# Experts two to four of a dense mixture on six tiles of 384 tokens in place of eight of 288

## The chip, the cores and the metric

One core of one Trainium2 chip runs the whole program. The metric is the device time of one execution in microseconds; lower is better. Several executions are timed and their median is given; one further execution was recorded by the hardware profiler, and every row below is from that one.

## The reference, cut to what matters

Three parts follow each other. B is 4 batches, S 576 tokens, 8 heads of 64; there are 2304 tokens of 512 features, E is 4 experts of width 1024, and the last layer has width 2048.

```
p_packed = attention(p, k, v)                # 32 packed queries a head
x = attention(q, p_packed, p_packed)         # 2304 x 512
p = domain_probs / (domain_probs.sum(-1) + 1e-9)
for e in range(4):                           # every token goes through every expert
    h = max(x @ w1[e], 0)
    out += p[:, e] * (h @ w2[e])
h = out @ w_in
g = P(h) / (Q(h) + 1e-6)                     # a cubic over a quadratic in |h|
y = g @ w_out
```

## The kernel before, in words

**Precision.** Each float32 operand of a large product is split into a rounded high part and a low part (both of the type fp32r), and a product is three matmuls: high by high, low weight by high, high by low.

**Folded weights.** The second attention's output is not formed. Its probabilities, 32 a head, are kept for all tokens in `aH` and `aL` (two groups of 128 rows, 2304 columns), and the packed values of a batch are multiplied into an expert's first weights. So the first product of expert e works with a weight `wb[e, bb]` that is different for each batch `bb`, and has two groups of 128 rows to sum over. `st_wb` (line 138) builds one half of such a weight (16 matmuls at line 147, a rounding copy by ScalarE at line 149) and `st_wbl` (line 134) its low part (VectorE, line 136). Two `wb` buffers exist; one accumulator area of two banks serves the builds (line 473).

**Units.** The expert stage is a list of 256 units (line 475): expert, batch, half of a batch (288 tokens), and one of eight chunks of 128 of the expert's width. For each unit `emit_h` (line 526) issues 6 matmuls of 288 columns into one of two banks (line 471): two groups by three. VectorE then applies the maximum with zero and the token's weight (line 558), ScalarE rounds (line 559), GpSimd forms the low part (line 560). Three units later `emit_out` (line 641) issues the second product of that unit, 12 matmuls of 288 columns (line 639): four accumulator banks, one for each 128 output features, by three. After eight chunks `emit_acc` (line 685) moves the four banks into the accumulator `acc` in SBUF: a copy by ScalarE for expert one, a sum by VectorE (line 695) for the others.

```
units = [("m", e, bb, a_, c) for e in range(E) for bb in range(B) for a_ in range(2) for c in range(NCH1)]
for i, (w, x) in enumerate(ops):
    nc.tensor.matmul(ps[:, :n], w, x, start=(i == 0), stop=(i == len(ops) - 1))
```

**Order.** All is written out by hand, one step a unit. A step's order on TensorE is: the first product of unit kk, then the second product of unit kk - 3, then whatever `at_step` (lines 512 to 517) put after it: the attention of the following batches and the builds of folded weights in expert one, then one build of two halves per batch, at the steps 4 and 10 of the 16 steps of a batch (line 516), each followed one step later by its low part. Beside this run the loading and splitting of the second weights (`put_w2`, line 119), of the token weights (`load_pw`, line 219, one row of 288 broadcast to all partitions, one tile ahead), and of the next expert's raw first weights.

**Conversion.** `w_in` and `w_out` come as 64-bit floats. `narrowing` (line 161) converts them in 32 tasks to two fp32r parts in DRAM; a task is cut in seven pieces: a load on SP's queue, four pieces with two VectorE instructions each (lines 193 to 205), one with a rounding by ScalarE and a subtraction by GpSimd, one with two stores. From step 41 on, two pieces are taken in each step (line 775), none in the steps where an accumulator is emptied or near a change of expert.

**Last stage.** 96 units of 384 tokens by 128 of the width of 2048: 12 matmuls of 384 columns (line 548), a chain over VectorE (lines 578, 579 and 592), ScalarE and GpSimd for the rational function, and four units later 9 matmuls of 512 columns (line 639). Its inputs are split from `acc` (`emit_x2`, line 701), its weights read back by `put_final` (line 128).

Of the kernel before, what the change touches and what calls it, by code (L numbers as in the profile page):

```python
# [8 lines left out]
F32 = mybir.dt.float32  # L9
F32R = mybir.dt.float32r  # L10
# [3 lines left out]
ALU = mybir.AluOpType  # L14
# [5 lines left out]
def kernel(ctx, tc, q, k, v, p, probs, w1, w2, w_in, a, b, w_out, out):  # L20
    nc = tc.nc
    B, H, S, D = q.shape
    NT, E = probs.shape
# [3 lines left out]
    P = 128  # L27
    KC = DM // P
# [3 lines left out]
    HALF = S // 2  # L32
    KP = 96
    NKC = S // KP
    NJ = NKC // 2
    TOK = 384
# [3 lines left out]
    NCH1 = F1 // P  # L40
    NCH2 = F2 // P
    FH = 512
    LAGF = 4

    const = ctx.enter_context(tc.tile_pool(name="const", bufs=1))
    wp = ctx.enter_context(tc.tile_pool(name="wp", bufs=NCH1))
    hp = ctx.enter_context(tc.tile_pool(name="hp", bufs=4))
# [5 lines left out]
    pwp = moe.enter_context(tc.tile_pool(name="pwp", bufs=2, side="right"))  # L53
# [4 lines left out]
    with tc.manual_schedule():  # L58
# [49 lines left out]
        wb = {}  # L108
# [108 lines left out]
        pw = {}  # L217

        def load_pw(n):

            if n < E * B * 2:
                w = pw[n] = pwp.tile([P, HALF], F32, tag="pw", name="pw")
                nc.sync.dma_start(out=w, in_=prow[n * NJ:(n + 1) * NJ, :].rearrange("(o s) n -> o (s n)", o=1).to_broadcast([P, HALF]))

# [245 lines left out]
        ps_acc = ctx.enter_context(tc.tile_pool(name="ps_acc", bufs=KC, space=PSUM, reuse_waits="tile"))  # L472
        apt = tc.tile_pool(name="apt", bufs=1, space=PSUM, side="right", reuse_waits="tile")
        banks[0] = apt.__enter__()
        units = [("m", e, bb, a_, c) for e in range(E) for bb in range(B) for a_ in range(2) for c in range(NCH1)]
        NUM = len(units)
        units += [("f", pr, c, tt) for pr in range(NPAIR) for c in range(NCH2) for tt in range(2)]
        NU = len(units)
        PH = 2 * NCH1


        side = {}

        def at_step(kk, w, f, *args):
            side.setdefault((kk, w), []).append((f, args))
# [25 lines left out]
        ATT = (B - 2) * PACE + 15  # L511
        for c in range(2, NCH1):
            at_step(c - 1, 1, put_w2, 0, c)
        for ph in range(B - 1, E * B - 1):
            for fh in range(2):
                at_step(ph * PH + 4 + 6 * fh, 1, st_wb, (ph + 1) // B, (ph + 1) % B, fh)
                at_step(ph * PH + 5 + 6 * fh, 0, st_wbl)
        tail = ExitStack()
        cvt = iter(())
        tp = None  # L520
# [5 lines left out]
        def emit_h(u):  # L526
            ps = ps_h.tile([P, 512], F32, tag="h", name="h")
            ops = []
            if u[0] == "m":
                _, e, bb, a_, c = u  # L530
                n = HALF
                w = wb[e, bb]
                cols = slice(bb * S + a_ * HALF, bb * S + (a_ + 1) * HALF)
                for g in range(2):
                    wh, wl = (w[:, x, g, c * P:c * P + P] for x in range(2))
                    ops += [(wh, aH[:, g, cols]), (wl, aH[:, g, cols]), (wh, aL[:, g, cols])]
            else:
                _, pr, c, tt = u
                n = TOK
                w = wts["f", pr * NCH2 + c, 0]  # L540
                xh, xl = xs[2 * pr + tt]
                for kc in range(KC):
                    wh, wl = (w[:, x, kc * P:kc * P + P] for x in range(2))
                    ops += [(wh, xh[:, kc, :]), (wl, xh[:, kc, :]), (wh, xl[:, kc, :])]
            if u == units[0]:
                keep(ps[:, :P], 44)
            for i, (w, x) in enumerate(ops):
                nc.tensor.matmul(ps[:, :n], w, x, start=(i == 0), stop=(i == len(ops) - 1))  # L548
            ph = ps[:, :n]
            if u[0] == "m":  # L550
                t = (e * B + bb) * 2 + a_
                if c == 0:
                    load_pw(t + 1)
                hw = hp.tile([P, HALF], F32, tag="hw", name="hw", bufs=2)
                hh = hp.tile([P, HALF], F32R, tag="hh", name="hh")
                hl = hp.tile([P, HALF], F32R, tag="hl", name="hl")
                hs[u] = (hh, hl)
                nc.vector.scalar_tensor_tensor(out=hw, in0=ph, scalar=0.0, in1=pw[t], op0=ALU.max, op1=ALU.mult)  # L558
                nc.scalar.copy(out=hh, in_=hw)  # L559
                nc.gpsimd.tensor_tensor(out=hl, in0=hw, in1=f32(hh), op=ALU.subtract)  # L560
                return
            m = tp.tile([P, TOK], F32, tag="m", name="m")
            c1 = tp.tile([P, TOK], F32, tag="c1", name="c1")
            c0 = tp.tile([P, TOK], F32, tag="c0", name="c0")
            nc.scalar.activation(out=c1, in_=ph, func=AF.Identity, scale=a_sb[:, 3:4], bias=a_sb[:, 2:3])
            nc.scalar.activation(out=m, in_=ph, func=AF.Abs, scale=b_abs[:, 0:1])
            nc.scalar.activation(out=c0, in_=ph, func=AF.Identity, scale=a_sb[:, 1:2], bias=a_sb[:, 0:1])

            nc.scalar.activation(out=ph, in_=ph, func=AF.Square)  # L569
            nc.scalar.activation(out=m, in_=m, func=AF.Identity, bias=one)  # L570
            mid[u] = (m, ph, c1, c0)
# [65 lines left out]
        def products(ps, n, ops, first, last):  # L637
            for i, (w, x) in enumerate(ops):
                nc.tensor.matmul(ps[:, :n], w, x, start=(first and i == 0), stop=(last and i == 2))  # L639

        def emit_out(u):
            hh, hl = hs.pop(u)
            if u[0] == "m":
                _, e, bb, a_, c = u
                wh, wl = (wts[e, c][:, x, :] for x in range(2))
                if c == 0:
                    accs["m"] = [ps_acc.tile([P, 512], F32, tag="acc", name="acc") for _ in range(KC)]
                for s, ps in enumerate(accs["m"]):
                    o = slice(s * P, s * P + P)

                    products(ps, HALF, ((wh[:, o], hh), (wh[:, o], hl), (wl[:, o], hh)), c == 0, c == NCH1 - 1)
                if c == NCH1 - 1:
                    late.append((u, accs["m"]))
            else:
                _, pr, c, tt = u
                wh, wl = (wts["f", pr * NCH2 + c, 1][:, x, :] for x in range(2))
                if c == 0:
                    accs[tt] = [(ps_y if tt and s else ps_acc).tile([P, 512], F32, tag="acc", name="acc") for s in range(SUB)]
                for s, ps in enumerate(accs[tt]):
                    o = slice(s * P, s * P + P)  # L660

                    products(ps, DM, ((hh[:, o], wh), (hl[:, o], wh), (hh[:, o], wl)), c == 0, c == NCH2 - 1)
                if c == NCH2 - 1:
                    late.append((u, accs[tt]))
# [20 lines left out]
        def emit_acc():  # L685
            while late:
                u, bks = late.pop(0)
                for s, ps in enumerate(bks):
                    if u[0] == "m":
                        _, e, bb, a_, c = u  # L690
                        dst = acc[bb][:, s, a_ * HALF:(a_ + 1) * HALF]
                        if e == 0:
                            nc.scalar.copy(out=dst, in_=ps[:, :HALF])
                        else:
                            nc.vector.tensor_tensor(out=dst, in0=ps[:, :HALF], in1=dst, op=ALU.add)
                        continue
                    store(u, s, ps)
                if u[0] == "m" and u[1] == E - 1:
                    done_cols[0] += HALF

        def emit_x2(t, bb, c0, n, o, kc):
            hi, lo = (x[:, kc:kc + 2, o:o + n] for x in xs[t])
# [21 lines left out]
        def refill(u, j):  # L724

            if u[0] == "m":
                _, e, bb, a_, c = u
                if j == 1 and bb == B - 1 and a_ == 1:
                    if e + 1 < E:
                        put_w2(e + 1, c)  # L730
                    else:
                        put_final(c // 2, c % 2)
            else:
                _, pr, c, tt = u
                n = pr * NCH2 + c + NCH1 // 2
                if tt == 1 and n < NPAIR * NCH2:
                    put_final(n, j)

        for kk in range(NU):
            if kk == ATT:  # L740
# [1 line left out]
                accp2 = ctx.enter_context(tc.tile_pool(name="accp2", bufs=1, reuse_waits="tile"))  # L742
                acc += [accp2.tile([P, KC, S], F32, name=f"acc{i}") for i in range(2, B)]
                cvt = narrowing(tail.enter_context(tc.tile_pool(name="cv", bufs=2, reuse_waits="tile")))
            if kk == NUM - 3 * PH:
                for _ in cvt:
                    pass
                tail.close()
                xp0 = ctx.enter_context(tc.tile_pool(name="xp0", bufs=1, reuse_waits="tile"))
                for t in range(2):  # L750
                    xs[t] = [xp0.tile([P, KC, TOK], F32R, name=f"x{nm}{t}") for nm in "HL"]
# [20 lines left out]
            emit_acc()  # L772


            for _ in range(0 if kk % NCH1 == 2 or (B * PH - 5 <= kk % (B * PH) or kk % (B * PH) < 5) else 2):
                next(cvt, None)
            if todo and todo[0][0] <= done_cols[0] and (kk < NUM or kk % 2 == 0) and todo[0][1][0] in xs:
                emit_x2(*todo.pop(0)[1])
# [43 lines left out]
```

## Time and profile before

| what | us |
|---|---|
| median of three executions | 1145.38 |
| lowest and highest of them | 1144.23, 1145.69 |
| the profiled execution, its own time | 1144.21 |
| its span, first to last instruction of the program | 1142.4 |
| TensorE's matmuls busy in the span | 1119.4 |
| VectorE, ScalarE, GpSimd busy | 756.6, 542.3, 628.5 |

In a row of the timeline the first number is the start in us from the span's start and the second the time from the first start to the last end of what was merged in that row; two starts are apart by that time less the duration of the last one. Matmuls overlap: one of 288 columns is shown with about 295 ns from its start to its modelled end, while its successor starts earlier. PE is the matmuls and PEld the weight loads, both on TensorE. "h" is the result of a first product, "acc" of a second, "wb" of a build of folded weights. Arrows in brackets name what ended the idle time before an instruction.

### The profile page before, as it was taken

How to read it: one execution, taken by the hardware profiler on the slowest of the kernel's cores; microseconds unless marked ns; L12 is line 12 of the kernel's file. 1: busy time of each engine (PE TensorE's matmuls, PEld its weight loads, DVE VectorE, ACT ScalarE, POOL GpSimd, SP SyncE). 2: the span in 40 equal slices, each digit the busy share in tenths (PEclk: the TensorE clock that was granted, in tenths of full speed). 3: DMA queues.
4: the chain of work that ended last, by engine and by line, in shares of the span. 5: the costliest groups of instructions: out<-in, count | busy, mean ns of one | idle time of the engine just before them, and what ended most of it. 6: DMA issues, size and time to landing. Idle time of an engine off the chain costs nothing.

```text
span 1142.4 us, 20688 instructions
## 1 busy us (share of the span) xinstructions
PE 1119.4 (98%) x8163; PEld 1025.5 (90%) x8163; DVE 756.6 (66%) x1061; ACT 542.3 (47%) x1085; POOL 628.5 (55%) x664
## 2 busy tenths in 40 slices
PE   8899999999999999999999999999999999999997
PEld 6678889999999999999999999988998999999996
DVE  3443436728888657878452332578888988888886
ACT  4443443342222332222322221577778777787774
POOL 0543434464445564444645333487877777777774
PEclk9899999999999999999999999999999999999999
DMA  9543214332344333344300000533333534354321
GB/s 259 132 125 88 69 48 127 129 98 89 113 153 145 103 113 116 106 153 133 112 25 11 6 7 6 186 111 120 137 113 122 191 119 138 113 169 144 125 98 55
DMA packets 61920, 125.93 MB, mean 110 GB/s; under 512 B 6960, under 2 KB 29488, under 8 KB 61824
## 3 DMA queue, kind: packets, MB, share of 16 engines
q1 hardware_dynamic: 61504, 123.79, 34.7%
q8 instruction: 64, 1.05, 0.4%
q0 software_dynamic: 320, 0.82, 0.2%
q14 instruction: 32, 0.26, 0.1%
HBM read 103.06 MB, written 21.53 MB: 109 GB/s over the span
## 4 chain that ended last, share of the span: by engine, by line
PE 91%; DVE 3%; ACT 2%; issue 2%; POOL 2%; POOLq 0%; ACTq 0%; DVEq 0%
PE acc L639 50%; PE h L548 34%; PE wb L147 3%; PE tr L293 1%; PE s L302 1%; DVE m L579 1%; PE e1t L327 1%; PE h L251 0%; PE pp L339 0%; POOL m L586 0%; POOL hl L601 0%; ACT e L315 0%; POOL c L593 0%; DVE mx L310 0%; PE pT L251 0%
## 5 line engine op out<-in xcount | busy, mean ns | idle before, releaser
L639 PE MATMUL acc<-hh,w 128*128 128x288 f32 x2048 | 449.6, 296 | 0.0
L560 POOL TENSOR_TENSOR hl<-hw,hh 128x288 fp32r<-128x288 f32 x256 | 211.7, 829 | 331.9 <-ACT hh L559 331.7
L639 PEld LDWEIGHTS acc<-hh,w 128*128 128x128 f32 x2048 | 341.5, 188 | 9.3 <-issue 9.3
L639 PE MATMUL acc<-hl,w 128*128 128x288 f32 x1024 | 301.1, 294 | 0.0
L559 ACT CAST hh<-hw 128x288 fp32r<-128x288 f32 x256 | 110.4, 431 | 381.3 <-DVE hw L558 379.4
L558 DVE SCALAR_TENSOR_TENSOR hw<-h,pw 128x288 f32<-128x288 f32 x256 | 116.1, 454 | 263.7 <-PE h L548 255.7
L579 DVE RECIPROCAL m<-m 128x384 f32<-128x384 f32 x95 | 242.5, 2553 | 3.2
L548 PE MATMUL h<-aH,wb 128*128 128x288 f32 x1024 | 216.9, 300 | 0.0
L548 PE MATMUL h<-xH,w 128*128 128x384 f32 x768 | 197.0, 337 | 3.0 <-DVE m L578 3.0
L639 PE MATMUL acc<-w,hh 128*128 128x512 f32 x576 | 194.8, 393 | 0.2 <-ACT hh L630 0.2
L639 PEld LDWEIGHTS acc<-hl,w 128*128 128x128 f32 x1024 | 192.4, 188 | 0.0
L548 PEld LDWEIGHTS h<-aH,wb 128*128 128x128 f32 x1024 | 163.1, 188 | 24.7 <-issue 10.7
L548 PEld LDWEIGHTS h<-xH,w 128*128 128x128 f32 x768 | 140.5, 188 | 13.0 <-DVE m L578 5.4
L548 PE MATMUL h<-aL,wb 128*128 128x288 f32 x512 | 151.4, 296 | 0.0
L586 POOL TENSOR_TENSOR m<-m,c 128x384 f32<-128x384 f32 x94 | 95.8, 1019 | 72.4 <-DVE m L579 72.4
L548 PE MATMUL h<-xL,w 128*128 128x384 f32 x384 | 129.5, 337 | 0.0
L639 PEld LDWEIGHTS acc<-w,hh 128*128 128x128 f32 x576 | 108.2, 188 | 21.2 <-ACT hh L630 0.7
L639 PE MATMUL acc<-w,hl 128*128 128x512 f32 x288 | 113.9, 396 | 0.0
L593 POOL TENSOR_TENSOR c<-c,c 128x384 f32<-128x384 f32 x96 | 97.9, 1020 | 5.2 <-DVE c L592 3.8
L601 POOL TENSOR_TENSOR hl<-m,hh 128x384 fp32r<-128x384 f32 x94 | 95.6, 1017 | 7.2 <-ACT hh L587 7.2
L548 PEld LDWEIGHTS h<-aL,wb 128*128 128x128 f32 x512 | 96.5, 188 | 0.1
L592 DVE TENSOR_TENSOR c<-h,c 128x384 f32<-128x384 f32 x96 | 52.5, 547 | 51.5 <-ACT h L569 51.4
(110 smaller groups left out, 1290.6 us busy)
## 6 DMA issues: line engine op xcount, KB each, us to landing
w<-nw SPq DMA_DIRECT2D x96, 512.0 KB, 4.2
r<-in_moe_w_dram SPq DMA_DIRECT2D x32, 256.0 KB, 2.7
raw<-in_moe_w_in_dram SPq DMA_DIRECT2D x16, 512.0 KB, 4.6
raw<-in_moe_w_out_dram SPq DMA_DIRECT2D x16, 512.0 KB, 3.8
nw<-raw SPq DMA_DIRECT2D x32, 256.0 KB, 2.3
nw<-t SPq DMA_DIRECT2D x32, 256.0 KB, 2.6
r<-in_moe_w_dram SPq DMA_DIRECT2D x7, 1024.0 KB, 5.6
pw<-prow SPq DMA_DIRECT2D x32, 144.0 KB, 3.7
```

What stands on the lines that cost most here:

```text
L147: nc.tensor.matmul(ps[32 * c:32 * c + 32, g, :], bd[r, 2 * bb + g, 32 * c:32 * c + 32], raw1[fh][r, c, f], start=True, stop=True, tile_pos ...
L293: nc.tensor.transpose(ps[:, hh, c * KP:c * KP + KP], src[2 * j + hh][:, c * 2 * D:(c + 1) * 2 * D], ident[:KP, :KP])
L548: nc.tensor.matmul(ps[:, :n], w, x, start=(i == 0), stop=(i == len(ops) - 1))
L558: nc.vector.scalar_tensor_tensor(out=hw, in0=ph, scalar=0.0, in1=pw[t], op0=ALU.max, op1=ALU.mult)
L559: nc.scalar.copy(out=hh, in_=hw)
L560: nc.gpsimd.tensor_tensor(out=hl, in0=hw, in1=f32(hh), op=ALU.subtract)
L579: nc.vector.reciprocal(out=m, in_=m)
L586: nc.gpsimd.tensor_tensor(out=m, in0=m, in1=c1, op=ALU.mult)
L592: nc.vector.tensor_tensor(out=c1, in0=s, in1=c1, op=ALU.mult)
L593: nc.gpsimd.tensor_tensor(out=c1, in0=c1, in1=c0, op=ALU.add)
L601: nc.gpsimd.tensor_tensor(out=hl, in0=m, in1=f32(hh), op=ALU.subtract)
L639: nc.tensor.matmul(ps[:, :n], w, x, start=(first and i == 0), stop=(last and i == 2))
```

## The change

The list of units is made from tiles of tokens: for expert one eight tiles of 288 as before, for each of the other three six tiles of 384 that don't keep to batches (`TOK` is 384, `HALF` 288, `S` 576, `NT` 2304). Tiles 1 and 4 of the six lie in two batches, 192 tokens in each; there the first product is two series of 6 matmuls with 192 columns, one with each batch's folded weight, into the two parts of one bank. Everything after that works on all 384 columns at once, but for the sum into `acc`, which is kept by batch. The builds of folded weights move to steps 3 and 5 of tiles 0, 2, 3 and 5. The conversion takes three pieces a step from expert two on.

```
+    tiles = [(0, c0, HALF) for c0 in range(0, NT, HALF)] + [(e, c0, TOK) for e in range(1, E) for c0 in range(0, NT, TOK)]
...
-            if n < E * B * 2:
-                w = pw[n] = pwp.tile([P, HALF], F32, tag="pw", name="pw")
-                nc.sync.dma_start(out=w, in_=prow[n * NJ:(n + 1) * NJ, :].rearrange("(o s) n -> o (s n)", o=1).to_broadcast([P, HALF]))
+            e, c0, m = tiles[n]
+            r0 = (e * NT + c0) // KP
+            w = pw[n] = pwp.tile([P, m], F32, tag="pw", name="pw")
+            nc.sync.dma_start(out=w, in_=prow[r0:r0 + m // KP, :].rearrange("(o s) n -> o (s n)", o=1).to_broadcast([P, m]))
...
-        units = [("m", e, bb, a_, c) for e in range(E) for bb in range(B) for a_ in range(2) for c in range(NCH1)]
+        units = [("m", n, c) for n in range(len(tiles)) for c in range(NCH1)]
         NUM = len(units)
+        begin = [NCH1 * [t[0] for t in tiles].index(e) for e in range(E)] + [NUM]
+
+        def pieces(n):
+
+            _, c0, w = tiles[n]
+            at, got = c0, []
+            while at < c0 + w:
+                k_ = min(c0 + w - at, S - at % S)
+                got.append((at // S, at % S, at - c0, k_))
+                at += k_
+            return got
...
-        for ph in range(B - 1, E * B - 1):
-            for fh in range(2):
-                at_step(ph * PH + 4 + 6 * fh, 1, st_wb, (ph + 1) // B, (ph + 1) % B, fh)
-                at_step(ph * PH + 5 + 6 * fh, 0, st_wbl)
+
+        for fh in range(2):
+            at_step((2 * B - 2) * NCH1 + 4 + 6 * fh, 1, st_wb, 1, 0, fh)
+            at_step((2 * B - 2) * NCH1 + 5 + 6 * fh, 0, st_wbl)
+        for e in range(1, E):
+            for n, e2, bb in ((0, e, 1), (2, e, 2), (3, e, 3), (5, e + 1, 0)):
+                for fh in range(2 if e2 < E else 0):
+                    at_step(begin[e] + n * NCH1 + 3 + 2 * fh, 1, st_wb, e2, bb, fh)
+                    at_step(begin[e] + n * NCH1 + 4 + 2 * fh, 0, st_wbl)
...
-                _, e, bb, a_, c = u
-                n = HALF
-                w = wb[e, bb]
-                cols = slice(bb * S + a_ * HALF, bb * S + (a_ + 1) * HALF)
-                for g in range(2):
-                    wh, wl = (w[:, x, g, c * P:c * P + P] for x in range(2))
-                    ops += [(wh, aH[:, g, cols]), (wl, aH[:, g, cols]), (wh, aL[:, g, cols])]
+                _, t, c = u
+                e, c0, n = tiles[t]
+                for bb, _, o, m in pieces(t):
+                    w = wb[e, bb]
+                    cols = slice(c0 + o, c0 + o + m)
+                    for g in range(2):
+                        wh, wl = (w[:, x, g, c * P:c * P + P] for x in range(2))
+                        ops += [(slice(o, o + m), g == 0 and i == 0, g == 1 and i == 2, wx, x)
+                                for i, (wx, x) in enumerate(((wh, aH[:, g, cols]), (wl, aH[:, g, cols]), (wh, aL[:, g, cols])))]
...
-            for i, (w, x) in enumerate(ops):
-                nc.tensor.matmul(ps[:, :n], w, x, start=(i == 0), stop=(i == len(ops) - 1))
+            for o, first, last, w_, x in ops:
+                nc.tensor.matmul(ps[:, o], w_, x, start=first, stop=last)
...
-                    products(ps, HALF, ((wh[:, o], hh), (wh[:, o], hl), (wl[:, o], hh)), c == 0, c == NCH1 - 1)
+                    products(ps, n, ((wh[:, o], hh), (wh[:, o], hl), (wl[:, o], hh)), c == 0, c == NCH1 - 1)
...
-                        dst = acc[bb][:, s, a_ * HALF:(a_ + 1) * HALF]
-                        if e == 0:
-                            nc.scalar.copy(out=dst, in_=ps[:, :HALF])
-                        else:
-                            nc.vector.tensor_tensor(out=dst, in0=ps[:, :HALF], in1=dst, op=ALU.add)
+                        for bb, at, o, n in pieces(u[1]):
+                            dst = acc[bb][:, s, at:at + n]
+                            if tiles[u[1]][0] == 0:
+                                nc.scalar.copy(out=dst, in_=ps[:, o:o + n])
+                            else:
+                                nc.vector.tensor_tensor(out=dst, in0=ps[:, o:o + n], in1=dst, op=ALU.add)
...
-            for _ in range(0 if kk % NCH1 == 2 or (B * PH - 5 <= kk % (B * PH) or kk % (B * PH) < 5) else 2):
+            for _ in range(0 if kk % NCH1 == 2 or any(-5 <= kk - x < 5 for x in begin[1:]) else 2 if kk < begin[1] else 3):
                 next(cvt, None)
```

The other lines of the diff rename what a unit is made of. The list has 208 units of the experts after the change, 64 of expert one and 48 of each other.

## Rows read from the trace of the kernel before

**Rows 1.** The page: busy time of TensorE, and the chain by engine.

```profile
PE 1119.4 (98%) x8163; PEld 1025.5 (90%) x8163; DVE 756.6 (66%) x1061; ACT 542.3 (47%) x1085; POOL 628.5 (55%) x664
...
PE 91%; DVE 3%; ACT 2%; issue 2%; POOL 2%; POOLq 0%; ACTq 0%; DVEq 0%
```

**Rows 2.** Busy time by stretch: expert two (instructions; PEclk, DMA share, GB/s last).

```profile
241.00:402.70 161.70, 161.70 (x1282) 153.70 (x1281) 120.10 (x210) 47.40 (x98) 82.48 (x86) 1.00 0.38 119
```

**Rows 3.** Waits of the weight loads, 241.06 to 723.7: total, times, longest.

```profile
PEld h L548 <- DVE acc L695: 9.2, 11, 0.8
PEld h L548 <- issue: 6.7, 8, 0.8
```

**Rows 4.** Timeline of TensorE's matmuls: experts two to four, and four units within.

```profile
241.06 0.43 PE L548 MATMUL h<-aH,wb 128*128 128x288 f32 x2
...
400.38 0.30 PE L548 MATMUL h<-aH,wb 128*128 128x288 f32 x1
...
409.88 0.29 PE L548 MATMUL h<-aH,wb 128*128 128x288 f32 x1
...
723.75 0.52 PE L548 MATMUL h<-xH,w 128*128 128x384 f32 x2
```

**Rows 5.** Groups by form, 241.06 to 723.7: busy, mean ns, idle before.

```profile
L147 PE MATMUL wb<-r,bd 64*32 64x512 f32 x352 | 24.0, 601 | 0.0
```

**Rows 6.** The chain in order of time, last stage: start, us.

```profile
787.35 2.10 PE h L548 x12
789.46 2.08 PE acc L639 x9
...
858.52 2.10 PE h L548 x12
```

**Rows 7.** Timeline of the weight loads: with nothing streaming, and in the stream.

```profile
26.96 0.20 PEld L251 LDWEIGHTS h<-ident 128*128 128x128 f32 x2 [0.51 <-PE s L302]
...
31.72 0.30 PEld L548 LDWEIGHTS h<-aH,wb 128*128 128x128 f32 x2
...
402.64 0.32 PEld L548 LDWEIGHTS h<-aH,wb 128*128 128x128 f32 x2
...
1135.12 0.19 PEld L639 LDWEIGHTS acc<-w,hl 128*128 128x128 f32 x1
1135.22 0.19 PEld L639 LDWEIGHTS acc<-w,hh 128*128 128x128 f32 x1
```

**Rows 8.** Groups by form, whole span: work beside TensorE.

```profile
L558 DVE SCALAR_TENSOR_TENSOR hw<-h,pw 128x288 f32<-128x288 f32 x256 | 116.1, 454 | 263.7 <-PE h L548 255.7 <-POOL t L378 2.6 <-POOL xL L705 1.9
...
L592 DVE TENSOR_TENSOR c<-h,c 128x384 f32<-128x384 f32 x96 | 52.5, 547 | 51.5 <-ACT h L569 51.4
...
L695 DVE TENSOR_TENSOR acc<-acc,acc 128x288 f32<-128x288 f32 x96 | 37.7, 450 | 0.0
L136 DVE TENSOR_TENSOR wb<-wb 128x1024 fp32r<-128x1024 f32 x31 | 37.5, 1211 | 3.4 <-ACT wb L149 3.4
...
L149 ACT CAST wb<-wb 128x1024 fp32r<-128x1024 f32 x31 | 31.5, 1016 | 33.3 <-PE wb L147 33.2
```

**Rows 9.** Timeline at the last stage's start: VectorE, then TensorE.

```profile
732.99 2.55 DVE L579 RECIPROCAL m<-m 128x384 f32<-128x384 f32 x1
735.46 1.49 DVE L695 TENSOR_TENSOR acc<-acc,acc 128x288 f32<-128x288 f32 x4
736.87 0.55 DVE L592 TENSOR_TENSOR c<-h,c 128x384 f32<-128x384 f32 x1
...
737.99 0.44 PE L548 MATMUL h<-xH,w 128*128 128x384 f32 x1 [1.01 <-DVE m L578]
```

**Rows 10.** Groups by form, whole span: VectorE's heavier pieces of the conversion.

```profile
L200 DVE SCALAR_TENSOR_TENSOR u<-u,t 128x512 int32<-128x512 int32 x32 | 29.9, 933 | 0.6
L205 DVE TENSOR_TENSOR u<-u,t 128x512 f32<-128x512 f32 x32 | 27.3, 852 | 1.1
...
L204 DVE SCALAR_TENSOR_TENSOR t<-raw,t 128x512 f32<-128x512 uint32 x32 | 23.2, 724 | 0.6
L202 DVE TENSOR_SCALAR t<-u 128x512 int32<-128x512 int32 x32 | 22.9, 714 | 1.1
```

More of the change, by code (lines that the diff above doesn't have):

```diff
@@ L474 @@
         banks[0] = apt.__enter__()
-        units = [("m", e, bb, a_, c) for e in range(E) for bb in range(B) for a_ in range(2) for c in range(NCH1)]
+        units = [("m", n, c) for n in range(len(tiles)) for c in range(NCH1)]
         NUM = len(units)
+        begin = [NCH1 * [t[0] for t in tiles].index(e) for e in range(E)] + [NUM]
[7 more added lines that the diff above has]
+            return got
         units += [("f", pr, c, tt) for pr in range(NPAIR) for c in range(NCH2) for tt in range(2)]
         NU = len(units)
-        PH = 2 * NCH1
         side = {}
@@ L543, in emit_h @@
                     wh, wl = (w[:, x, kc * P:kc * P + P] for x in range(2))
-                    ops += [(wh, xh[:, kc, :]), (wl, xh[:, kc, :]), (wh, xl[:, kc, :])]
+                    ops += [(slice(0, n), kc == 0 and i == 0, kc == KC - 1 and i == 2, w_, x)
+                            for i, (w_, x) in enumerate(((wh, xh[:, kc, :]), (wl, xh[:, kc, :]), (wh, xl[:, kc, :])))]
             if u == units[0]:
                 keep(ps[:, :P], 44)
-            for i, (w, x) in enumerate(ops):
-                nc.tensor.matmul(ps[:, :n], w, x, start=(i == 0), stop=(i == len(ops) - 1))
+            for o, first, last, w_, x in ops:
+                nc.tensor.matmul(ps[:, o], w_, x, start=first, stop=last)
             ph = ps[:, :n]
             if u[0] == "m":
-                t = (e * B + bb) * 2 + a_
-                if c == 0:
+                if c == 0 and t + 1 < len(tiles):
                     load_pw(t + 1)
-                hw = hp.tile([P, HALF], F32, tag="hw", name="hw", bufs=2)
-                hh = hp.tile([P, HALF], F32R, tag="hh", name="hh")
-                hl = hp.tile([P, HALF], F32R, tag="hl", name="hl")
+                hw = hp.tile([P, n], F32, tag="hw", name="hw", bufs=2)
+                hh = hp.tile([P, n], F32R, tag="hh", name="hh")
+                hl = hp.tile([P, n], F32R, tag="hl", name="hl")
                 hs[u] = (hh, hl)
@@ L643, in emit_out @@
             if u[0] == "m":
-                _, e, bb, a_, c = u
+                _, t, c = u
+                e, _, n = tiles[t]
                 wh, wl = (wts[e, c][:, x, :] for x in range(2))
@@ L689, in emit_acc @@
                     if u[0] == "m":
-                        _, e, bb, a_, c = u
-                        dst = acc[bb][:, s, a_ * HALF:(a_ + 1) * HALF]
-                        if e == 0:
-                            nc.scalar.copy(out=dst, in_=ps[:, :HALF])
-                        else:
-                            nc.vector.tensor_tensor(out=dst, in0=ps[:, :HALF], in1=dst, op=ALU.add)
+                        for bb, at, o, n in pieces(u[1]):
[4 more added lines that the diff above has]
+                                nc.vector.tensor_tensor(out=dst, in0=ps[:, o:o + n], in1=dst, op=ALU.add)
                         continue
                     store(u, s, ps)
-                if u[0] == "m" and u[1] == E - 1:
-                    done_cols[0] += HALF
+                if u[0] == "m" and tiles[u[1]][0] == E - 1:
+                    done_cols[0] += tiles[u[1]][2]
         def emit_x2(t, bb, c0, n, o, kc):
@@ L726, in refill @@
             if u[0] == "m":
-                _, e, bb, a_, c = u
-                if j == 1 and bb == B - 1 and a_ == 1:
+                _, t, c = u
+                e, c0, n = tiles[t]
+                if j == 1 and c0 + n == NT:
                     if e + 1 < E:
@@ L744 @@
                 cvt = narrowing(tail.enter_context(tc.tile_pool(name="cv", bufs=2, reuse_waits="tile")))
-            if kk == NUM - 3 * PH:
+            if kk == begin[E - 1] + 2 * NCH1:
                 for _ in cvt:
```

## The prediction

> **What bounds the kernel now.** I read the page first, for the engine that is never idle. TensorE is busy for 98% of the span and carries 91% of the chain that ended last [rows 1], so what its stream of products takes is what the program takes, as long as nobody keeps it waiting. Second I read the three experts that the change touches, as stretches: in the first of them TensorE is busy for all of its 161.70 us at a granted clock of 1.00, which is the 2.4 GHz level, while VectorE has 120.10 us of work, three quarters [rows 2]. Third the waits: TensorE's matmuls wait for nobody in the three experts, and the weight loader's longest pauses, 0.8 us [rows 3], stand where the eight-part products of the folded weights stream and no load is due. So this stage is a pure stream, and the question is what one product in it costs.
>
> That is read from the timeline. Experts two to four run from the first product of expert two at 241.06 to the first of the last stage at 723.75, 482.69 us [rows 4]. Four units of 18 products with 288 columns go from 400.38 to 409.88 [rows 4], 2.375 us a unit, 131.9 ns a product; 192 units make 456.0 us. The other 26.7 us are the 22 builds of folded weights (352 products, 16 each [rows 5]), 1.21 us each.
>
> The last stage gives a second point. A unit there is 12 products of 384 columns and 9 of 512, and 17 such units go from 787.35 to 858.52 in the chain [rows 6], 4.1865 us each. With a product's time as a + b times its columns, 18a + 5184b = 2.375 and 21a + 9216b = 4.1865 give b = 0.447 ns and a = 3.2 ns. So a product of 384 columns takes 174.8 ns (the 2.10 us shown for twelve of them [rows 6] agree), and one of 192 would take 89.0 ns if only its columns counted. A product's fixed share is tiny, 3 ns: fewer, wider products have little to win.
>
> **What the row of the weight loads adds.** Each product has its own load of 128 columns ahead of it. In the stream the loads start 0.13 us apart (two in 0.32 us, one lasting 0.19 [rows 7]), at the pace of the products, so this doesn't show what a load needs. It shows where nothing streamed: at 31.72 two loads start 0.11 us apart (two in 0.30 us, one lasting 0.19 [rows 7]), though only the first product was to start in between. From there to the pair at 1135.12 [rows 7] 94 pairs are so, at 107 to 111 ns to the nanosecond, 109 in the mean. The second load can't start until the first product has taken over the first weights, and that product is waiting for them: about 109 ns is what one load occupies. For 288 columns (132 ns) and more it is hidden behind the product before it. For 192 (89 ns) it isn't. The nearest row for a cheaper load is that of the plain transposes at 26.96, where the second starts 0.06 us after the first [rows 7]; those load the identity unrounded, in the transposing mode, and the products of the experts don't.
>
> **The change part by part.**
>
> *Products.* Before: 192 units of 18, 3456 products of 288, 456.0 us. After: each of three experts has six tiles of eight units. Four tiles lie in one batch: 18 products of 384. Two lie across a boundary: 12 of 192 in the first product, 12 of 384 in the second. That makes 2304 of 384, 2304 x 174.8 ns = 402.8 us, and 576 of 192. Bounds of a halved product: 89 ns by columns, 111 ns by the slowest pair of loads; I take 109 ns, since the rows of the same kind of load all say so, and 107 to 111 for the range. 576 x 109 ns = 62.8 us. Sum 465.6 us, **+9.6 us** (+8.4 to +10.7). Counting columns alone it would be 454.1 us, -1.9 us.
>
> By the Trainium skill ("TensorE: Matmul & The Clock Gate", Back-to-back issue gap) the spacing of warm matmuls is the columns over 2.4 GHz plus 2.5 ns, and a sustained stream of load and matmul pairs still makes 81 ns at 128 columns; both would put 192 columns well below 109 ns. Its formula gives 122.5 ns for 288 columns where the trace has 131.9, and by it the products would take 421.9 us in place of 423.4, a gain of 1.5 us. No run here shows its case of 128 columns with a load ahead of each.
>
> *Builds of folded weights.* 22 before and after (eight for expert two, eight for three, six for four), at other steps: no change. The two halves come two units apart where they were six, and share one bank: the second must wait until ScalarE and VectorE have read the first, 1.02 and 1.21 us [rows 8], with two units of over 3.1 us to do it in. If the cover went, each of 11 second halves would pay up to that, 2.2 us.
>
> *Vector work per unit.* The weighting goes from 64 instructions of 454 ns an expert to 48 at about 0.55 us (547 ns for another one of 384 columns [rows 8]), the cast and the subtraction likewise. The sum into the accumulator is four of 0.55 us in a plain tile, eight of about 0.35 us (from 450 ns at 288 columns and 547 at 384 [rows 8], 1 ns a column) in a split one, 2.8 us where 1.8 stood. It starts bank by bank while the last second product still runs (2.1 us) and the next tile's first second product comes after a first product of 1.05 us or more, so each bank is free 1 us ahead: hidden. If not, 6 tiles x 0.5 us = 3 us.
>
> *Conversion of the last stage's weights.* Three pieces a step in place of two from expert two on, in steps of 3.1 us in place of 2.4: the same load, to within a tenth, on an engine with a quarter free [rows 2]. It ends earlier, by the end of expert three. A raw tile is loaded again only after its predecessor was stored, and three steps, 9.4 us, lie between; on SP's queue the rows of token weights (one load a tile, of 384 now and then, ahead by one tile of 25 us) stand behind no more than before, and nothing else there is moved but the raw first weights, which have two tiles. Cost 0, up to +3.
>
> *Entry of the last stage.* The last three second products of expert four run between the first units of that stage: 3 x 12 x 43 ns = +1.5 us, already in the sum. VectorE is busy there: a reciprocal from 732.99 to 735.5, then the four sums into the accumulator from 735.46, then the next unit's work at 736.87, and TensorE's next product at 737.99 after 1.01 us idle [rows 9]. After the change the second products end at 12.6 us from the stage's start where they ended at 11.0, and the reciprocal at 12.3 in place of 11.8, since its unit's first product comes 0.5 later; the four sums (2.2 us, bank by bank) end at 14.5, and with 1.05 us for the next two vector instructions the product starts at 15.5 where it started at 14.24: +1.3 for +1.5. So -0.25 us, from -1.5 (all swallowed) to +1.
>
> Sum: **+9.3 us**. The profiled execution took 1144.21 us, 1.2 under the median of the three runs, 1145.38; that makes 1153.5 for it and **1154.7 us** for the median, 0.8% slower. What counts as a difference at all is 0.2%, 2.3 us.
>
> **Rivals.**
> - *The load stays hidden, not slower (0.10).* If a load can begin while the one before it is still waiting to be used, halves cost 89 ns: -1.9 - 0.25, 1143.2 us, on the edge between no change and faster. It decides at the 576 halves, and at 109 ns against 89. For it: the straight line through 288, 384 and 512 columns. Against it: 94 pairs that never start closer than 107 ns with an empty array. The Trainium skill's sustained 81 ns at 128 columns (same page and section) is this rival.
> - *VectorE's queue takes over (0.05).* The first product of a unit needs the bank that was read by the weighting two units back; from the end of one first product there are 2.10 + 1.05 + 2.10 = 5.25 us. Three pieces of conversion, two of them 0.93 + 0.71 and 0.72 + 0.85 us [rows 10] and a third at most like the lighter of these, make 4.8 us, with the weighting 5.35, and 1.2 us of folded weights on top in 16 steps of experts two and three. If each of those kept TensorE waiting for 0.8 us, 13 us more: 1167.5 us. Against it: three quarters of load, and after a heavy bunch come pieces with no vector work.
> - That the halves be merged again can't be: they have different weights.
>
> **How the numbers follow.** Forecast 0.85, first rival 0.10 (of which 0.07 within 0.2% and 0.03 faster by more), second 0.05. Slower by over 0.2%: 0.85 + 0.05 = 0.90. The range holds the forecast's case alone: low end +8.4 - 1.3 at the entry, 1152.5; high end +10.7 + 1 at the entry and some 1.4 of queueing, 1158.5. The first rival's time lies outside, with 0.10, and the second's with 0.05.
>
> **What would show it.** Halved products 107 to 111 ns apart, a split unit at 3.40 us and a plain one at 3.15 us; experts two to four at 492 us in place of 482.7; TensorE still without a wait there; and the stretch from the last stage's start to its fifth unit longer by 1.3 us. Halves 89 ns apart would make the forecast wrong, as would pauses of TensorE ahead of a first product that VectorE ends.

## The result, and the profile after

The change takes 1155.11 us in the median of five runs (1153.81 to 1156.35) where the kernel before takes 1145.69 us in five runs beside it: a ratio of 1.0082 (95% interval 1.0071 to 1.0093), slower. The forecast was 1154.7 us, between 1152.5 and 1158.5. In a later set the two stood at 1153.95 and 1145.47 us, 1.0071 (1.0059 to 1.0084).

The profiled execution took 1156.35 us with a span of 1154.5, 12.1 more than before. Of these 2.7 lie ahead of everything that was changed: the first product of expert one started at 34.5 us where it had started at 31.7, and in the eleven profiles of this study it lies anywhere from 31.7 to 34.8, with nothing altered ahead of it but sizes of buffers and, in three of the runs, one load of raw weights. In this execution 1.9 of the 2.7 are 44 transposes just ahead of that product: they start 0.11 us apart before, and here for a good part 0.21, in a stretch where the granted clock is 0.50 (27.75 to 31.70), which is the level of 1.2 GHz. So I compare stretches, not spans. These are the ends of the stretch that was changed (timeline of TensorE's matmuls of the changed kernel; they answer to [rows 4] and [rows 9]):

```profile
243.22 0.51 PE L570 MATMUL h<-aH,wb 128*128 128x384 f32 x2
...
734.00 0.51 PE L570 MATMUL h<-xH,w 128*128 128x384 f32 x2
...
749.14 0.45 PE L570 MATMUL h<-xH,w 128*128 128x384 f32 x1 [0.41 <-DVE m L599]
```

Experts two to four take 490.78 us in place of 482.69, +8.1. From their start to the fifth unit of the last stage, where the last three second products are done as well, it is 505.92 us in place of 496.93 (241.06 to 737.99): **+9.0 us**. The rest, +3.1 in this execution, is the start and half a microsecond either way elsewhere.

Where the 9 us are is seen in the chain in order of time, at the step from a plain tile to a split one (start, us, instructions):

```profile
266.22 1.04 PE h L570 x6
267.26 2.08 PE acc L660 x12
269.34 1.32 PE h L570 x12
270.66 2.12 PE acc L660 x12
272.77 1.32 PE h L570 x12
```

A plain unit takes 3.12 us, for 18 products of 384 columns. A split one takes 3.44, for 12 of 192 and 12 of 384: the same columns, 0.32 us more, and there are 48 of them. The timeline of the weight loads at the start of that split unit shows the cause (two loads in 0.30 us, one lasting 0.19):

```profile
269.40 0.30 PEld L570 LDWEIGHTS h<-aH,wb 128*128 128x128 f32 x2
269.62 0.19 PEld L570 LDWEIGHTS h<-aL,wb 128*128 128x128 f32 x1
269.74 0.30 PEld L570 LDWEIGHTS h<-aH,wb 128*128 128x128 f32 x2
```

The loads come 0.11 us apart, the distance that [rows 7] showed with nothing streaming: here the products wait for them. The timeline puts such a wait on the product behind it: the first half of a series is shown with 0.09 us and the first wide product behind a series with 0.20, but the distance of the loads is the same, 0.11, all through. VectorE has 128.62 us of work in expert two where it had 120.10 [rows 2], in a stretch that is 1.6 us longer, at the same granted clock (busy time by stretch):

```profile
243.22:406.50 163.28, 163.28 (x1091) 154.58 (x1090) 128.62 (x198) 45.79 (x83) 78.84 (x71) 1.00 0.37 125
```

One wait has come that was not there: 0.5 us of the weight loader, once, for ScalarE's rounding of a weighted product (waits of the weight loads from 243 to 734; the first row answers to [rows 3]):

```profile
PEld h L570 <- issue: 18.4, 22, 0.8
...
PEld acc L660 <- ACT hh L580: 0.5, 1, 0.5
```

### The profile page after: what moved, and what is told of

Same layout as the page of the kernel before. It is cut to its first block, busy times and chain, and to the rows that moved or that the text cites. A ratio compares the mean times of both kernels' runs of the same rounds, so it can differ in the third digit from the quotient of the medians.

```text
span 1154.5 us, 19370 instructions
## 1 busy us (share of the span) xinstructions
PE 1129.3 (98%) x7587; PEld 1032.7 (89%) x7587; DVE 768.6 (67%) x1013; ACT 534.6 (46%) x1037; POOL 618.3 (54%) x616
## 4 chain that ended last, share of the span: by engine, by line
PE 87%; DVE 4%; ACT 3%; POOL 2%; issue 2%; DMA 1%; SPq 0%; POOLq 0%; DVEq 0%; ACTq 0%
PE acc L660 47%; PE h L570 33%; PE wb L150 3%; PE tr L297 1%; DVE m L600 1%; DMA b_sb<-in_moe_b_dram 1%; POOL m L607 1%; PE s L306 1%; POOL hl L622 1%; PE h L255 1%; POOL c L614 1%; PE pp L343 0%; PE e1t L331 0%; DVE hw L579 0%; ACT c L586 0%
## 5 line engine op out<-in xcount | busy, mean ns | idle before, releaser
L660 PE MATMUL acc<-hh,w 128*128 128x384 f32 (+1 forms) x1664 | 432.2, 325 | 0.2 <-ACT hh L580 0.2
L581 POOL TENSOR_TENSOR hl<-hw,hh 128x384 fp32r<-128x384 f32 (+1 forms) x208 | 202.3, 972 | 337.7 <-ACT hh L580 337.4
L660 PEld LDWEIGHTS acc<-hh,w 128*128 128x128 f32 x1664 | 295.7, 188 | 10.0 <-issue 9.2
L579 DVE SCALAR_TENSOR_TENSOR hw<-h,pw 128x384 f32<-128x384 f32 (+1 forms) x208 | 108.8, 523 | 258.3 <-PE h L570 246.0
L580 ACT CAST hh<-hw 128x384 fp32r<-128x384 f32 (+1 forms) x208 | 101.4, 488 | 376.0 <-DVE hw L579 374.0
L660 PE MATMUL acc<-hl,w 128*128 128x384 f32 (+1 forms) x832 | 267.9, 322 | 0.0
L570 PE MATMUL h<-aH,wb 128*128 128x192 f32 (+2 forms) x1024 | 221.8, 306 | 0.0
L570 PEld LDWEIGHTS h<-aH,wb 128*128 128x128 f32 x1024 | 169.9, 190 | 24.7 <-issue 22.5
L660 PEld LDWEIGHTS acc<-hl,w 128*128 128x128 f32 x832 | 156.5, 188 | 0.0
L570 PE MATMUL h<-aL,wb 128*128 128x384 f32 (+2 forms) x512 | 155.0, 303 | 0.0
```

Of the source, the lines that this page charges most:

```text
L570: nc.tensor.matmul(ps[:, o], w_, x, start=first, stop=last)
```

## The experiments

The theory is the forecast's: a product lasts as long as its columns or as the load of 128 weight columns behind it, whichever is longer, and only the halves are shorter than a load. Against it stand a fixed cost of some 20 ns for every product of a piece; a limit that bites only in a long series of short products; a cost of having two folded weights in a unit; and VectorE's queue. Each kernel was timed against the kernel before.

**The halves taken away.**

```
-                for bb, _, o, m in pieces(t):
+                for bb, _, o, m in ([(c0 // S, 0, 0, n)] if e else pieces(t)):
```

> The change as it is, but a tile that lies in two batches makes its first product in one series of 6 with 384 columns, with the folded weight of its first batch for both parts (so half of its columns get the wrong batch's weight). Theory (a halved product is bound by its weight load, 109.5 ns measured, where 384 columns take 173.4): a split unit's first product goes from 1.314 to 1.040 us, 48 units, 13.1 us less than the change: 1142.0 us, and experts two to four at 477.7 us. This is also what the wider tiles alone are worth against the kernel before: -3.7 us. Rival (part of the loss comes from the vector engines' queues, the builds or the entry of the last stage): it stays, so the time is over 1145 us.

Measured: 1142.96 us, 0.9981 (0.9971 to 0.9991); experts two to four 476.8 us. The split unit costs what a plain one does (chain in order of time):

```profile
266.96 2.08 PE acc L660 x12
269.04 1.04 PE h L570 x6
270.08 2.08 PE acc L660 x12
```

So the whole loss of the stretch is in the halves: without them 384 columns are 5.9 us better there than 288. Of this 2.4 us are left between the medians; in the profiled execution 0.9 us go at the entry of the last stage and 1.9 in the program's start, which varies from profile to profile.

**More halves.** Both runs cut the first products of the plain tiles, too, with the same weights for both parts; the first in 192 and 192 columns (K = 192), the second in 96 and 288 (K = 96).

```
-                for bb, _, o, m in pieces(t):
+                for bb, _, o, m in ([(p_[0], 0, p_[2] + y, z) for p_ in pieces(t) for y, z in ((0, K), (K, TOK - K))]
+                                    if e and len(pieces(t)) == 1 else pieces(t)):
```

> The change, with the first product of the plain tiles of experts two to four cut in two series of 192 columns too, same weights in both. Theory of the load: 96 more units go from 1.040 to 1.314 us, +26.3 us: 1181.4 us, twice the number of halved products at the same 109.5 ns. Rival one (a product of a half costs some 20 ns on top of its columns, whatever they are: new group, new region of the bank): the same +26. Rival two (the loss has to do with two different folded weights in one unit): no loss here but the 3 ns of each further product, +1.8 us: 1156.9 us.

> As the cut in 192 and 192, but the plain tiles are cut in 96 and 288 columns: the same number of products and loads. Theory of the load: 288 columns (131.9 ns) hide it, 96 columns don't and take 109.5 ns, so a unit's first product takes 6 x 241.4 ns = 1.448 us, +39.2 us: 1194.3 us, 13 us more than the cut in halves. Rival one (20 ns on top of the columns for each product of a cut): 6 x (46 + 132 + 40) ns = 1.308 us, +25.7 us: 1180.8 us, the same as the cut in halves.

Measured: 1184.64 us (1.0344, 1.0329 to 1.0360) and 1195.76 us (1.0441, 1.0426 to 1.0457). The second cut has the same number of products and loads and the same columns, yet costs 11 us more: a product of 96 columns takes the 0.11 us of a load as one of 192 does, and one of 288 takes its own 0.13. A fixed cost for each piece would have made the two equal, and two folded weights in a unit are not needed for the loss, since here both parts have the same. The first came out 3 us over the theory, which the chain shows as 2.12 us in place of 2.08 for the second products behind each cut unit, 96 x 0.04. In the run with 96 columns the first product of a plain unit is (timeline):

```profile
259.78 0.32 PE L570 MATMUL h<-aH,wb 128*128 128x96 f32 x2
259.94 0.27 PE L570 MATMUL h<-aL,wb 128*128 128x96 f32 x1
260.05 0.39 PE L570 MATMUL h<-aH,wb 128*128 128x96 f32 x2
260.27 0.27 PE L570 MATMUL h<-aL,wb 128*128 128x96 f32 x1
260.38 0.50 PE L570 MATMUL h<-aH,wb 128*128 128x288 f32 x2
```

From the third product (259.94) to the sixth (260.27) it is 0.33 us, 0.11 a product: 96 columns cost what 192 do.

**A shorter load.**

```
+                r_ = slice(0, P if first or last or o.stop - o.start != TOK // 2 else P // 2)
-                nc.tensor.matmul(ps[:, o], w_, x, start=first, stop=last)
+                nc.tensor.matmul(ps[r_, o], w_[:, r_], x, start=first, stop=last)
```

> The change, but in each series of 6 products with 192 columns the middle four load and use only 64 of the 128 weight columns (they leave out half of the outputs of these four). Theory of the load: a load of 64 columns takes about half of 109 ns, which is less than the 87 to 89 ns of the product's columns; a product lasts the longer of its columns and the next load, so four of six (the first to the fourth) fall from 109.5 to 88 ns: 8 x 21.5 ns x 48 units = 8.3 us less: 1146.8 us. Rival one (a fixed 20 ns for each product of a half): 1155.1 us.

Measured: 1146.45 us, 1.0011 (1.0002 to 1.0020). The products keep their 192 columns and become cheaper as the load behind them does (timeline; 128*64 is a load of 64 columns):

```profile
267.17 0.34 PE L571 MATMUL h<-aH,wb 128*128 128x192 f32 x2
267.35 0.25 PE L571 MATMUL h<-aL,wb 128*64 128x192 f32 x1
267.43 0.34 PE L571 MATMUL h<-aH,wb 128*64 128x192 f32 x2
267.61 0.27 PE L571 MATMUL h<-aL,wb 128*128 128x192 f32 x1
267.72 0.37 PE L571 MATMUL h<-aH,wb 128*128 128x192 f32 x2
```

The first five products of this series take 0.44 us (267.17 to 267.61), 88 ns each, which is what 192 columns were to cost if only they counted (89 ns). The sixth and the first of the next series take 0.11 each. Which load is behind which product is seen in the loads themselves (timeline of the weight loads; the row at 267.63 merges a full load with one of 64 columns 0.11 later):

```profile
267.26 0.13 PEld L571 LDWEIGHTS h<-aL,wb 128*64 128x64 f32 x1
267.35 0.22 PEld L571 LDWEIGHTS h<-aH,wb 128*64 128x64 f32 x2
267.52 0.19 PEld L571 LDWEIGHTS h<-aL,wb 128*128 128x128 f32 x1
267.63 0.25 PEld L571 LDWEIGHTS h<-aH,wb 128*128 128x128 f32 x2
267.83 0.14 PEld L571 LDWEIGHTS h<-aL,wb 128*64 128x64 f32 x1
```

From the start of a load of 64 columns it is 0.09 us to the next load (267.26, 267.35, 267.43, 267.52), from the start of a full one 0.11 (267.52, 267.63, 267.74). This also answers a rival that the edit itself brings in, that a product gets cheaper because it has only 64 outputs. A load starts with the product ahead of its own, as at 267.35 in both views, so from 267.52 to 267.63 the fifth product runs, which has 64 outputs and a full load behind it: 0.11. From 267.74 to 267.83 the first of the next series runs, which has 128 outputs and a load of 64 columns behind it: 0.09.

**The order changed.**

```
+            if u[0] == "m" and len(pieces(u[1])) > 1 and done + lag(done) <= kk:
+                mix = out_ops(units[done])
+                early.add(units[done])
-            for o, first, last, w_, x in ops:
+            for k_, (o, first, last, w_, x) in enumerate(ops):
                 nc.tensor.matmul(ps[:, o], w_, x, start=first, stop=last)
+                if mix:
+                    a2, w2_, x2, f2, l2 = mix[k_]
+                    nc.tensor.matmul(a2, w2_, x2, start=f2, stop=l2)
```

> The change, with the 12 halved first products of a split unit set one by one between the 12 second products (384 columns) that follow them. Theory of the load, with one set of weights held in reserve: a halved product still lasts as long as the load of the product behind it, 109.5 ns, and a product of 384 columns has time to spare for one load only; no order helps: 1155.1 us, within 1.5. Rival (loads can run ahead by more than one, and only a long series of short products uses the lead up): up to 576 x 21 ns = 12 us less, 1143 us.

Measured: 1165.78 us, 1.0176 (1.0162 to 1.0189), 11 us over what I expected. The products are as the theory has them: a pair of a short and a long one takes 0.285 us (two of them from 269.02 to 269.59), as they do one kind behind the other, 0.110 + 0.173 (timeline):

```profile
269.02 0.25 PE L574 MATMUL h<-aH,wb 128*128 128x192 f32 x1
269.11 0.36 PE L577 MATMUL acc<-hl,w 128*128 128x384 f32 x1
269.30 0.25 PE L574 MATMUL h<-aL,wb 128*128 128x192 f32 x1
269.39 0.36 PE L577 MATMUL acc<-hh,w 128*128 128x384 f32 x1
269.59 0.25 PE L574 MATMUL h<-aH,wb 128*128 128x192 f32 x1
```

What I had not reckoned with is that the order takes from the vector engines the time between a first product and the second product that needs it. TensorE now stands ahead of second products (its waits from 245 to 734):

```profile
PE acc L577 <- ACT hh L587: 6.1, 6, 1.1
PE acc L667 <- ACT hh L587: 3.6, 3, 1.4
```

These are 9.7 us of the 10.4 by which experts two to four got longer (501.2 us). No part of the loss came back by this order; and at six of the second products that it moved up by one first product (1.3 us) the vector engines were late, as they were at three in plain units.

**Pieces that hide the load.** If a piece must last longer than a load, the tile that lies in two batches should be the wide one: 320, 512 and 320 tokens for two batches, with pieces of 256.

```
-    ... [(e, c0, TOK) for e in range(1, E) for c0 in range(0, NT, TOK)]
+    ... [(e, c0 + d, m) for e in range(1, E) for c0 in range(0, NT, 2 * S) for d, m in ((0, 320), (320, 512), (832, 320))]
...
-                hw = hp.tile([P, n], F32, tag="hw", name="hw", bufs=2)
+                hw = hp.tile([P, n], F32, tag="hw", name="hw", bufs=1)
```

> Experts two to four on tiles of 320, 512 and 320 tokens in every two batches, so that the tile in two batches has pieces of 256; all other products have 320 or 512 columns, and there are as many products and loads as in the change. (To make room the buffers of the weighted product are one, of the raw second weights two, and some areas are given out at other times; the run beside it has these alone.) Theory of the load: 256 columns take about 117 ns, over the 109.5 of a load, so nothing is exposed: a pair of batches and chunk take 36 x 145.7 + 12 x 231.3 + 12 x 117 ns = 9.43 us where the change has 9.63, 48 of them, 9.7 us less: 1145.4 us, experts two to four at 481 us against 482.7 before, so 0 to 2 us under the kernel before. Rival one (20 ns for every product of a piece): 576 x 20 ns more, 1157 us.

> The change with the other uses of memory of the run with pieces of 256 (one buffer for the weighted product, two for the raw second weights, areas given out at other times) and its own tiles of 384. None of these is on TensorE's path: as the change, 1155.1 us within 1.5.

> The change itself beside the others: 1155.1 us, ratio 1.0082 to the kernel before.

Measured: 1153.05 us (1.0062, 1.0050 to 1.0074) with the new tiles, 1156.94 us (1.0097, 1.0084 to 1.0111) with the other uses of memory alone, 1153.95 us (1.0071) for the change itself. The products fit: 12 of 256 columns take 1.44 us, 120 ns each. But experts two to four took 488.5 us, not 481. The waits tell why; the longest is 1.9 us at 335.76, behind a bunch of conversion on VectorE, ScalarE and GpSimd, and the granted clock falls behind it, from 1.00 to a mean of 0.60 in the four microseconds from 335, which is the level of 1.2 GHz for most of them (first the waits of the matmuls from 245 to 734):

```profile
PE acc L660 <- ACT hh L580: 3.5, 2, 1.9
PE acc L660 <- DVE acc L717: 2.0, 3, 1.1
```

The longest of them in the timeline, with what came before it:

```profile
332.39 1.30 POOL L216 TENSOR_TENSOR t<-u,raw 128x512 fp32r<-128x512 f32 x1 [2.53 <-ACT raw L215]
...
333.65 1.04 POOL L581 TENSOR_TENSOR hl<-hw,hh 128x320 fp32r<-128x320 f32 x1
...
334.72 0.49 DVE L579 SCALAR_TENSOR_TENSOR hw<-h,pw 128x320 f32<-128x320 f32 x1 [0.75 <-POOL hl L581]
...
335.76 0.55 PE L660 MATMUL acc<-hh,w 128*128 128x320 f32 x1 [1.89 <-ACT hh L580]
```

GpSimd's piece of the conversion puts off its subtraction for the unit before, and VectorE's weighting stands 0.75 us for that subtraction, since the weighted product now has one buffer. So by the kernel's text the bunch and the one buffer both have a part in this wait; these tiles were not run with two buffers.

Busy time by stretch just there (the granted clock is third from the end):

```profile
331.00:335.00 4.00, 2.87 (x20) 2.60 (x18) 3.17 (x5) 0.98 (x2) 2.29 (x2) 1.00 0.46 173
335.00:339.00 4.00, 3.24 (x12) 3.12 (x12) 3.97 (x9) 0.92 (x2) 1.73 (x2) 0.60 0.57 155
```

The run with the memory changes alone shows that they aren't free either: its experts two to four are 1.9 us longer than the change's, with waits of the same kind (1.1 us in three, where the change has one of 0.2; for the weight loader 2.7 in five, where the change has one of 0.5). It took 3.0 us more than the change beside it; my expectation for it was 2 us too low.

**The same with the conversion spread by the length of a step.**

```
-            for _ in range(0 if ... else 2 if kk < begin[1] else 3):
+            for _ in range(0 if ... else 3 if kk < NUM and tiles[units[kk][1]][2] > TOK else 2):
```

> The run with pieces of 256, where TensorE stood for 8.0 us in experts two and three (five waits ahead of a second product, and one stretch at half clock behind the longest of them), with the conversion at three pieces only in the steps of the tiles of 512 columns and at two in the shorter steps. Theory (its products are as forecast, and the loss is VectorE's queue: three pieces of conversion do not fit a step of 320 columns): the waits of 1.7 to 2.1 us go and with them the half clock, the shorter ones behind a tile of 512 columns may stay: 1145 to 1148 us. Rival (the wider tiles themselves are what comes late): 1153 us as before.

Measured: 1145.93 us, 1.0004 (0.9995 to 1.0013), experts two to four 481.8 us. The matmuls' waits on ScalarE are gone, though the weighted product still has one buffer, and of the ones behind a tile of 512 columns 0.8 us are left:

```profile
PE acc L660 <- DVE acc L717: 0.8, 2, 0.5
```

This is 9 us better than the change and the same as the kernel before. No version tried here beats that clearly; the one with 0.9981 computes something else.

## Why the prediction was right

**The bound.** That experts two to four are a stream of products with nothing to wait for, read from [rows 1] to [rows 3], held: 0.5 us of waiting in 491. The mechanism, that halves last as long as a load and every other product as long as its columns, is what the runs show.

**The halved product.** 109 ns were forecast from pairs of loads [rows 7]; twelve take 1.32 us in the chain, 110 ns, and the second products behind them another 0.035 us a unit, so about 112 to 113 ns all told. "With an empty array" was said too broadly: at 89 of the 94 pairs a matmul is still shown in flight, as at 31.72, where the last transpose had only just started. The five without one are 108 to 109 ns apart too, so the reading stands. The transposes that run up to 31.72, and the first of these five (timeline of the weight loads of the kernel before):

```profile
26.96 4.78 PEld L251 LDWEIGHTS h<-ident 128*128 128x128 f32 x44 [0.51 <-PE s L302]
...
737.99 0.30 PEld L548 LDWEIGHTS h<-xH,w 128*128 128x128 f32 x2 [1.33 <-DVE m L578]
```

The first of these rows also sets two sentences of the prediction right. Only the first two of the 44 loads of the transposes start 0.06 us apart; all 44 take 4.78 us, 0.11 apart, so that row shows no cheaper load in a stream. And it is a stream of 128 columns with a load ahead of each, though of unrounded numbers, which the prediction said no run had.

The three runs that change the columns, the load and the number of such products agree with a load that is exposed, and with none of the other causes. The rule that a sustained pair at 128 columns takes 81 ns (the Trainium skill, "TensorE: Matmul & The Clock Gate", Back-to-back issue gap) doesn't hold for these loads: products of only 96 columns, with a load of 128 columns each, take 110 ns. The rival that went with it would have given 89 ns for a half.

**The wide product.** 174.8 ns were taken for 384 columns, from a line through this stage's 288 and the last stage's mixture. A plain unit shows 3.12 us for 18, 173.3 ns. Both errors are small and go opposite ways: plain units 96 x (3.120 - 3.146) = -2.5 us, split ones 48 x (3.440 - 3.406) = +1.6. The products cost 96 x 3.12 + 48 x 3.44 = 464.6 us, +8.6 in place of +9.6.

**Builds, sums, conversion.** Costed at nothing. The 16 products of a build took as long as before, 1.02 us, but the first product behind a build is 0.13 us longer than its like where it was 0.10 longer: 0.7 us in all 22, which had no term. Why is open. The conversion's bound of 0 to 3 us was right in its sign: 0.5 us of one wait. The experiments show that this cover was thinner than I wrote: second products moved up by one first product (10 us lost) or steps cut to 2.6 us with one buffer less (7 us lost, 488.5 against 481.8) use it up. My figure of three quarters of load says nothing of bunches.

**The entry of the last stage.** +1.3 us were forecast from its start to its fifth unit, and 15.14 us in place of 14.24 are +0.9; the four sums take 1.89 us where 2.2 were put. The mechanism is the one in [rows 9], with the four sums now of 384 columns behind a reciprocal (VectorE's timeline):

```profile
743.74 2.55 DVE L600 RECIPROCAL m<-m 128x384 f32<-128x384 f32 x1
746.21 1.89 DVE L717 TENSOR_TENSOR acc<-acc,acc 128x384 f32<-128x384 f32 x4
748.01 0.55 DVE L613 TENSOR_TENSOR c<-h,c 128x384 f32<-128x384 f32 x1
```

**The sum.** +9.3 us were forecast, +9.0 are in that stretch, and +9.4 and +8.5 between the medians of the two sets. In the list of what would show it I put experts two to four at 492 us; they took 490.8. That figure was careless: by my own working 1.5 us of the second products fall behind the last stage's start, which makes 490.8. That the sum came out so close is in part luck: the products were 1.0 us less than forecast and the entry 0.4 less, the builds and the one wait 1.0 more than nothing, and the program's start alone moves by 3.1 us between profiles. The low end of the range was added up with -1.3 at the entry where the bound given there is -1.5, which would make 1152.3.

## What to carry to other kernels

Before cutting a matmul's columns, look for what a weight load takes: two loads at the start of a run, the second right behind the first. Here a product shorter than that cost the load, in a long series and between long products alike, and widening the others didn't pay for it. When steps change their length, deal out by time the side work that was dealt out per step; an average load of three quarters says nothing of a bunch.

## What the runs showed that I had not expected

The fixed share of a product is not 3 ns. In the run with pieces of 256, spread conversion, 12 products of 256 columns start at 272.27, 12 of 320 at 273.71, and the next unit at 275.47 (timeline):

```profile
272.27 0.40 PE L570 MATMUL h<-aH,wb 128*128 128x256 f32 x2
...
273.71 0.31 PE L660 MATMUL acc<-hh,w 128*128 128x320 f32 x1
...
275.47 0.40 PE L570 MATMUL h<-aH,wb 128*128 128x256 f32 x2
...
281.65 0.40 PE L660 MATMUL acc<-hh,w 128*128 128x512 f32 x1
...
284.39 0.40 PE L570 MATMUL h<-aH,wb 128*128 128x256 f32 x2
```

That is 120 and 146.7 ns: 0.417 ns a column, one column at 2.4 GHz, and 13 ns on top; 384 columns with 173.3 fit too, 288 with 131.9 lie 1.4 ns below, and 512 in this stream (twelve from 281.65 to 284.39, 228 to 229 ns) lie about 2 above. My line came out steeper and with less on top since it rests on the last stage's products of 512 columns, with other operands, which cost 231 ns (nine in 2.08 us [rows 6]): about 4 more than this line has, and 2 to 3 more than 512 columns cost here. It cost the forecast 1.5 ns a product of 384 columns. Why the two streams differ was not tried.
